# Fewer split units in the last batch, and later summaries by block transposes with a common maximum

## The chip, the cores and the metric

The kernel runs on one core of a Trainium2 chip. The metric is the device time of one execution in microseconds (us); the median of three runs is given.

## What is computed

An attention block with 32 inducing points summarizes each of 4 batches of 12480 tokens, the tokens attend to that summary, and a two-layer network with a squared, clipped activation follows. All in float32, C = 128, d_ff = 2048; the reference, cut:

```python
B, N, m, C = (4, 12480, 32, 128)
def mab(q, kv):
    s = scale * (q @ kv.transpose(0, 2, 1))
    s = s - s.max(-1, keepdims=True)
    a = np.exp(s)
    a /= a.sum(-1, keepdims=True) + 1e-09
    return a @ kv
h = mab(I, x)            # 32 inducing points over all tokens of a batch
x = mab(x, h)            # each token over the 32 rows of h
h = x @ w_in             # 128 -> 2048
g = np.where(h >= 1, h, np.where(h <= -1, 0.0, (h + 1) ** 2 / 4))
out = g @ w_out          # 2048 -> 128
```

## The kernel before

A batch is cut into 26 chunks of 480 tokens, and chunks into groups of four (the seventh group has two). There are three kinds of work.

**Summary of a batch** (`summarize`). For each group PE computes the scores of the 32 points against the chunks' transposed tokens `xT`, four chunks side by side in the 128 partitions of one PSUM bank (`scores`, L554). DVE takes the maximum of each partition (`most`, L559) and scales it (`nb`, L562), ACT takes exponentials with that bias and their sums (`exps`, L571). PE then turns the exponentials in 4 transposes (`turn`, L595), ACT or DVE copies them to `eN` (`put`, L603), and PE multiplies them with the tokens `xn` in 16 tiled matmuls (`weigh`, L611), each chunk for itself; `keep` (L618) stores the 128 x 128 partial results. A short chain (`c1` to `c12`) joins the groups with a weight per partition and group, and `hT`, the summary, is multiplied with `w_in` (L720) into `hw`. Batch 0 is summarized at the start, from tokens that PE transposes itself, in 5 pieces of 96; the summary of batch b+1 is made while batch b's chunks run. There SP loads each chunk twice: as `xn`, and as `xr`, which a DVE block transpose makes into `xT` (L535).

**Attention of the tokens** (`attend`, L765 to L831): scores against `hT`, a softmax by DVE, ACT and POOL, and the weights `a` and their rounded part `ahi` are sent by SP to `aT`, four DMAs per chunk.

**The network** (`chunk`). A chunk has 8 units of 256 hidden columns, each in two PSUM banks of pool `h` (7 banks). Per unit: two hidden matmuls (L953, one pass each, float32r), ReLU on ACT (L961; one wide instruction if both banks are ready and adjacent, or two single ones), square on ACT (L947), the cap on DVE (L966; pair or single). The output matmul (L1053) runs in one of two ways. A *split* unit makes `hi`, a rounded copy of `w` (on DVE L1024, ACT L1021 or POOL L1019, as the planner chooses), and `lo = w - hi` on POOL (L1027), and PE runs three single-pass matmuls per half. Another unit uses `w` itself in a float32 matmul per half, which the trace shows as two records. `SPLIT` names the six split units of a chunk, `END` the five of the last chunk of all. DVE turns the sum (L1065) and SP stores it.

**Order.** No engine's order is written by hand. `Plan.order` runs a list of operations with costs through a model of the engines: at each step an engine takes, of the operations that are ready and whose buffers are free, the one with the lowest due time. Due times are a base (the unit's place times `STEP`) plus an entry of the table `DUE`; `LONE`, `KEEP` and `WAIT` are further constants of that choice, and `SLOTS` gives the number of buffers. The result is a fixed order for each engine's queue. Idle places of PE in the first 73 us of the plan are filled with small matmuls (`keep_on`, L1082). The score bank of a group is one of the seven `h` banks; it is free again after the exponentials:

```python
m = add("PE", 850, 1050, SC[0], scores, [ind_made, *(xT_made[b, c] for c in cs)],
        [p1, e1[g], *(xT[b, c] for c in cs)], tiled=True)
v = add("DVE", 760, 900, SC[1], most, [m, folded, prior], [p1])
mosts.append(v)
e = add("ACT", 645, 780, SC[2], exps, [v], [e1[g], p1])
```

Of the kernel before, what the change touches and what calls it, by code (L numbers as in the profile page):

```python
# [9 lines left out]
F32 = mybir.dt.float32  # L10
# [8 lines left out]

END = (0, 1, 3, 4, 6)  # L20
# [4 lines left out]
    h=7, o=1, xn=9, xT=26, xr=2, e1=1, eN=1, hw=6, hx=1, hy=1, w=8, hi=4, lo=4, aT=3, s2=2, a=1, ahi=1, oT=1  # L25
)

FIRST = ["xn", "w", "xn", "hi", "xn", "w", "xn", "lo", "xn", "w"]
# [22 lines left out]
    "end": [-102350],  # L51
# [19 lines left out]
LONE = {"r": 7750, "t": 3200}  # L71

KEEP = 100

WAIT = 175250
# [177 lines left out]
def attn_moe(  # L253
# [10 lines left out]
    P = 128  # L264
# [19 lines left out]
    SHAPE = [(5, 96)] + [(4, 120)] * (B - 1)  # L284
    x_first = x.rearrange("b (k p t) c -> b k p t c", p=96, t=5)
    x_rows = x.rearrange("b (k t p) c -> b k p t c", p=120, t=4)
# [4 lines left out]
        xn=([96, 5, C], F32), xT=([C, CW], F32),  # L291
# [4 lines left out]
    banks = psum.tile([P, SLOTS["h"] + SLOTS["o"], 512], F32, name="banks")  # L296
    count = [0]

    def make(slot, shape=None, dtype=None):

        count[0] += 1
        if slot.pool in ("h", "o"):
            slot.tile = banks[:, slot.place + (SLOTS["h"] if slot.pool == "o" else 0), :]
            return slot.tile
# [182 lines left out]
    def summarize(b, begin, pace, end):  # L487

        xn, got, e1, eN = {}, {}, {}, {}
        T, TP = SHAPE[b]  # L490
        rows_of = x_rows if b else x_first
        lasts, mosts, summed = [], [], []
        prior = state.get("chain")

        def load(g, due, step):
            for q in range(nqs[g]):
                c = g * Q + q
                due += step
                xT[b, c] = in_turn("xT")

                pool = FIRST[c % len(FIRST)] if b == 0 else "xn"
                xn[c] = in_turn(pool) if pool == "xn" else Slot(pool)
                got[c] = add(
# [4 lines left out]
                if b == 0:  # L508
                    pt = Slot("h")

                    def turn(c=c, pt=pt):
                        p = make(pt)
                        for t in range(T):
                            nc.tensor.transpose(  # L514
                                p[:, t * TP : (t + 1) * TP], xn[c].tile[:, t, :], ident[:TP, :TP]
                            )
# [621 lines left out]
```

## Time and profile before

| | |
|---|---|
| median of 3 runs | 1732.59 us (1731.34 to 1733.43) |
| the profiled execution | 1732.11 us, of which the trace spans 1730.3 |
| busy in the span | PE 1696.6 (98%), ACT 1664.2 (96%), DVE 1626.2 (94%), POOL 1612.6 (93%) |
| granted TensorE clock | 0.999 of full speed |
| DMA | 105.76 MB, mean 61 GB/s |

PE is TensorE's matmuls, PEld its weight loads, DVE VectorE, ACT ScalarE, POOL GpSimd, SP the engine that issues the DMAs, SPq its queue. L12 is line 12 of the kernel. An instruction's duration includes its way through the engine, which the next one overlaps; what an instruction costs a full engine is read from its start to the next one's start. A name such as `w` stands for all buffers of that pool.

### The profile page before, as it was taken

To read this page: it belongs to the slowest core of one execution; us is meant where nothing else is said; L and a number is where in the kernel's file an instruction comes from. 1 tells how busy PE (TensorE), PEld (TensorE's weight loads), DVE (VectorE), ACT (ScalarE), POOL (GpSimd) and SP (SyncE) were. 2 spreads that over 40 slices of the span, in tenths; PEclk is the share of its full clock that TensorE was granted. 3 is DMA by queue.
4 is the path that set the end of the run, shared out by engine and by line. 5 is a ranking of instruction groups with operands and counts; after the bars stand their busy time and mean duration, and the time that the engine had idled before them with its cause. 6 is when DMAs were issued, how large, how long until landed. Compare 5 with 4: busy or idle time off the path is not lost.

```text
span 1730.3 us, 26049 instructions
## 1 busy us (share of the span) xinstructions
PE 1696.6 (98%) x8062; PEld 1229.5 (71%) x8062; DVE 1626.2 (94%) x2167; ACT 1664.2 (96%) x2486; POOL 1612.6 (93%) x875
## 2 busy tenths in 40 slices
PE   6999999999999999999999999999999999999998
PEld 5667777777767777777777777777777677777776
DVE  5799999999999999999999999999999999999997
ACT  5699999999999999999999999999999999999997
POOL 1599999999899999999999999999989999999997
PEclk9999999999999999999999999999999999999999
DMA  9443323333334233343143333232212111111111
GB/s 235 112 74 69 74 58 70 57 62 61 70 66 77 47 72 63 66 75 68 31 93 54 74 68 69 51 66 52 42 34 53 33 30 30 35 35 35 33 31 18
DMA packets 427950, 105.76 MB, mean 61 GB/s; under 512 B 370562, under 2 KB 421218, under 8 KB 427810
## 3 DMA queue, kind: packets, MB, share of 16 engines
q1 hardware_dynamic: 426722, 103.84, 30.5%
q8 instruction: 64, 1.05, 0.3%
q14 instruction: 76, 0.62, 0.1%
q10 hardware_dynamic: 1088, 0.25, 0.1%
HBM read 48.94 MB, written 25.56 MB: 43 GB/s over the span
## 4 chain that ended last, share of the span: by engine, by line
PE 62%; ACT 16%; DVE 11%; issue 5%; POOL 3%; DMA 2%; SPq 1%; DVEq 0%; ACTq 0%; POOLq 0%
PE banks L1053 43%; PE banks L953 14%; ACT w L961 8%; ACT w L947 6%; DVE w L966 6%; DVE hi L1024 3%; POOL lo L1027 2%; PE banks L611 1%; PE banks L765 1%; ACT hi L1021 1%; PE banks L554 1%; SPq L532 1%; DMA xr<-in_x 1%; DVE oT L1065 1%; PE banks L514 1%
## 5 line engine op out<-in xcount | busy, mean ns | idle before, releaser
L1027 POOL TENSOR_TENSOR lo<-w,hi 128x960 fp32r<-128x960 f32 x623 | 1395.9, 2271 | 40.3 <-DVE hi L1024 17.9
L966 DVE SCALAR_TENSOR_TENSOR w<-banks,w 128x480 f32<-128x480 f32 (+1 forms) x1200 | 960.6, 838 | 35.9 <-ACT w L947 30.7
L961 ACT ACTIVATE w<-banks 128x480 f32<-128x480 f32 (+1 forms) x1352 | 843.7, 700 | 15.0 <-PE banks L953 13.9
L947 ACT ACTIVATE w<-w 128x960 f32<-128x960 f32 x832 | 842.2, 1049 | 2.7
L953 PE MATMUL banks<-aT,hw 128*128 128x480 f32 x1664 | 605.6, 432 | 7.3 <-DVE w L966 5.2
L1053 PE MATMUL banks<-hi,w_lo 128*128 128x480 f32 x1246 | 492.0, 395 | 5.4 <-DVE oT L1065 3.3
L1024 DVE TENSOR_REDUCE hi<-w 128x960 fp32r<-128x960 f32 x409 | 464.7, 1142 | 18.2 <-PE banks L1053 1.2
L1053 PE MATMUL banks<-hi,w_hi 128*128 128x480 f32 x1246 | 472.9, 380 | 0.0
L953 PEld LDWEIGHTS banks<-aT,hw 128*128 128x128 f32 x1664 | 304.7, 188 | 167.6 <-DVE w L966 71.1
L1053 PE MATMUL banks<-w,w_f 128*128 128x480 f32 x836 | 391.4, 567 | 0.0
L1053 PE MATMUL banks<-lo,w_hi 128*128 128x480 f32 x1246 | 385.2, 395 | 0.8 <-POOL lo L1027 0.8
L1053 PEld LDWEIGHTS banks<-hi,w_lo 128*128 128x128 f32 x1246 | 234.2, 188 | 76.2 <-DVE oT L1065 18.0
L1053 PEld LDWEIGHTS banks<-lo,w_hi 128*128 128x128 f32 x1246 | 229.8, 188 | 76.2 <-POOL lo L1027 25.7
L1053 PEld LDWEIGHTS banks<-hi,w_hi 128*128 128x128 f32 x1246 | 234.2, 188 | 40.0 <-issue 7.2
L1053 PEld LDWEIGHTS banks<-w,w_f 128*128 128x128 f32 x836 | 155.9, 189 | 68.7 <-issue 50.9
L1019 POOL TENSOR_SCALAR hi<-w 128x960 fp32r<-128x960 f32 x140 | 139.6, 1002 | 19.3 <-DVE w L966 10.4
L1021 ACT CAST hi<-w 128x960 fp32r<-128x960 f32 x74 | 75.5, 1021 | 4.7 <-DVE w L966 3.1
L1065 DVE STREAM_TRANSPOSE oT<-banks 128x480 f32<-128x480 f32 x104 | 70.1, 674 | 7.9 <-PE banks L1053 6.5
L535 DVE STREAM_TRANSPOSE xT<-xr 128x480 f32<-128x480 f32 x78 | 51.2, 659 | 0.0
L808 POOL TENSOR_TENSOR a<-a,ahi 128x480 fp32r<-128x480 f32 (+1 forms) x28 | 34.5, 1232 | 0.6 <-ACT ahi L805 0.6
L441 POOL TENSOR_TENSOR w_in_sb<-hi,lo 128x256 f32<-128x256 f32 x8 | 6.1, 763 | 28.4 <-DVE hi L430 28.4
L611 PEld LDWEIGHTS banks<-xn,eN 120*32 120x32 f32 (+1 forms) x754 | 24.4, 109 | 11.1 <-ACT eN L603 4.4
(107 smaller groups left out, 580.0 us busy)
## 6 DMA issues: line engine op xcount, KB each, us to landing
out<-oT SPq DMA_DIRECT2D x414, 60.0 KB, 2.2
xn<-in_x SPq DMA_DIRECT2D x91, 240.0 KB, 4.2
xr<-in_x SPq DMA_DIRECT2D x312, 60.0 KB, 2.5
aT<-ahi SPq DMA_DIRECT2D x206, 60.0 KB, 2.0
aT<-a SPq DMA_DIRECT2D x206, 60.0 KB, 2.0
w<-in_moe_w_in SPq DMA_DIRECT2D x8, 256.0 KB, 5.7
w<-in_moe_w_out SPq DMA_DIRECT2D x8, 256.0 KB, 3.8
hw<-hy SPq DMA_DIRECT2D x32, 64.0 KB, 2.0
```

What stands on the lines that cost most here:

```text
L535: nc.vector.transpose(make(xT[b, c]), xr.tile.rearrange("c n i -> c (n i)"))
L611: nc.tensor.matmul(p[q * M : (q + 1) * M, :C], eN[g].tile[:, t, q * M : (q + 1) * M], xn[g * Q + q].tile[:, t, :], start=(t == 0), stop=(t ...
L947: nc.scalar.activation(w.tile, w.tile, AF.Square, scale=0.5)
L953: nc.tensor.matmul(make(h)[:, :CW], hw[b][ft // 4].tile[:, ft % 4 * P : (ft % 4 + 1) * P], aT[b, c].tile, start=True, stop=True,)
L961: each(of, i, hs_, lambda h, to: nc.scalar.activation(to, h, AF.Relu, bias=1.0), w)
L966: lambda h, t: nc.vector.scalar_tensor_tensor(h if kept else t, h, 1.0, t, op0=ALU.max, op1=ALU.min), w,
L1019: nc.gpsimd.tensor_scalar(make(hi), w.tile, 1.0, 0.0, op0=ALU.mult, op1=ALU.add)
L1021: nc.scalar.copy(make(hi), w.tile)
L1024: nc.vector.tensor_reduce(make(hi), w.tile.unsqueeze(3), axis=AX.X, op=ALU.max)
L1027: nc.gpsimd.tensor_sub(make(lo), w.tile, hi.tile.bitcast(F32))
L1053: nc.tensor.matmul(acc.tile[:, :CW], wt[k][:, i, :], g.tile[:, i, :], start=first, stop=(acc.parts == 0),)
L1065: nc.vector.transpose(make(oT).rearrange("c n i -> c (n i)"), acc.tile[:, :CW])
```

## The change

1. In the last batch every chunk whose number is odd uses the five split units of `END` and three float32 units (unit 7 is the third). This holds for 13 chunks, of which the last had it before.
2. The later summaries turn the exponentials by 32 x 32 blocks on DVE, from SBUF to SBUF. For that the four chunks of a group must share one maximum per inducing point, since a matmul now sums over all four: DVE's maximum of each partition goes by four small DMAs (`line`) to 32 partitions, DVE takes the maximum of four (`one_most`), and four DMAs (`spread`) bring it back. The tokens are loaded by the same rows as the blocks, four chunks in one tile, and the weighted sum is 15 tiled matmuls.
3. The tokens' buffers: three of 128 x 1920 elements in place of nine of 96 x 640, the first batch's nine lying inside them; loads for later batches wait for the first summary's end.
4. The whole table `DUE` and the constants `LONE`, `KEEP` and `WAIT` have other numbers.

```diff
+LESS = ((), (), (), (1, 3))
 END = (0, 1, 3, 4, 6)
...
-    "h": [-28300, -9600, -120350, -9950, -10750, -3800, -56800, -49450],
+    "h": [-32350, -5700, -18700, -12450, -27300, -2200, -49100, -47200],
...
-LONE = {"r": 7750, "t": 3200}
-KEEP = 100
-WAIT = 175250
+LONE = {"r": 6200, "t": 800}
+KEEP = 800
+WAIT = 210850
...
+                    got[c] = add("SP", 700, 3000, at(due, "x"), fetch, state["first"], [xn[c]])
...
+            def line(q):
+                nc.sync.dma_start(m4[:, q : q + 1], mq[q * M : (q + 1) * M])
+            def one_most():
+                nc.vector.tensor_reduce(m4[:, Q:], m4[:, :nq], axis=AX.X, op=ALU.max)
+            def spread(q):
+                nc.sync.dma_start(mg[q * M : (q + 1) * M, g : g + 1], m4[:, Q:])
...
+                l = [add("SP", 610, 2700, SC[1], lambda q=q: line(q), [v]) for q in range(nq)]
+                v = add("DVE", 75, 215, SC[1], one_most, l)
+                l = [add("SP", 610, 2700, SC[1], lambda q=q: spread(q), [v, prior]) for q in range(Q)]
+                mosts.extend(l)
+                v = add("DVE", 75, 215, SC[1], less, l)
...
+                def over():
+                    to = make(eN[g], [P, NB, M])[:rows].rearrange("p n m -> p (n m)")
+                    nc.vector.transpose(to, e1[g].tile[:rows])
+                def weigh_all():
+                    p = make(ph)
+                    for n in range(NB):
+                        nc.tensor.matmul(
+                            p[n % Q * M : (n % Q + 1) * M, :C], eN[g].tile[:rows, n, :], xn[g * Q].tile[:rows, n, :],
+                            start=n < Q, stop=n >= NB - Q,
+                        )
...
-            split = k in (END if (b, c) == (B - 1, NCH - 1) else SPLIT)
+            split = k in (END if (b, c) == (B - 1, NCH - 1) or c % 4 in LESS[b] else SPLIT)
```

Two places of the order. The first is PE at the end of the first summary, ahead of the turns of its sixth group (`ident` alone: a filler; `ident,e`: the turns; `xT,indT`: the scores of the last group). Before:

```order
L611 MATMUL banks<-xn_435,eN_776 32x128
L611 MATMUL banks<-lo_376,eN_776 32x128
L611 MATMUL banks<-xn_445,eN_776 32x128
L611 MATMUL banks<-w_412,eN_776 32x128
L1082 MATMUL banks<-ident 128x128 x11
L595 MATMUL banks<-ident,e_161_835 96x128 x5
L554 MATMUL banks<-xT_759,indT 32x480
L554 MATMUL banks<-xT_770,indT 32x480
L611 MATMUL banks<-xn_463,eN_851 32x128
```

Changed:

```order
L670 MATMUL banks<-tokens,eN_812 32x128
L670 MATMUL banks<-lo_426,eN_812 32x128
L670 MATMUL banks<-tokens,eN_812 32x128
L670 MATMUL banks<-w_462,eN_812 32x128
L1139 MATMUL banks<-ident 128x128 x21
L655 MATMUL banks<-ident,e_158_893 96x128 x5
L571 MATMUL banks<-xT_795,indT 32x480
L571 MATMUL banks<-xT_806,indT 32x480
L670 MATMUL banks<-tokens,eN_911 32x128
```

Ten more fillers stand between the fifth group's weighted sum and the sixth group's turns; what follows is the same.

The second is DVE around the maximum of the second group of batch 1's summary, made while batch 0 runs (`mg<-banks` and `nb<-mg` before; now `mq<-banks`, and the maximum of four is `m_1_1`). Before:

```order
L1024 TENSOR_REDUCE hi_2037<-w_1985 128x960
L1024 TENSOR_REDUCE hi_2047<-w_1993 128x960
L559 TENSOR_REDUCE mg<-banks 128x1
L562 TENSOR_SCALAR nb_1_120<-mg 128x1
L966 SCALAR_TENSOR_TENSOR w_2021<-banks,w_2021 128x480 x2
L966 SCALAR_TENSOR_TENSOR w_2049<-banks,w_2049 128x960
L1065 STREAM_TRANSPOSE oT_2079<-banks 128x480
L966 SCALAR_TENSOR_TENSOR w_2007<-banks,w_2007 128x480 x2
L1024 TENSOR_REDUCE hi_2096<-w_2049 128x960
L603 COPY eN_2108<-banks 120x512
```

Changed:

```order
L1023 SCALAR_TENSOR_TENSOR w_2002<-banks,w_2002 128x480 x2
L577 TENSOR_REDUCE mq_1_138<-banks 128x1
L1081 TENSOR_REDUCE hi_2059<-w_1986 128x960
L1023 SCALAR_TENSOR_TENSOR w_2033<-banks,w_2033 128x480
L1023 SCALAR_TENSOR_TENSOR w_2048<-banks,w_2048 128x960
L1023 SCALAR_TENSOR_TENSOR w_2033<-banks,w_2033 128x480
L1023 SCALAR_TENSOR_TENSOR w_2071<-banks,w_2071 128x480
L1081 TENSOR_REDUCE hi_2096<-w_2048 128x960
L586 TENSOR_REDUCE m_1_1_139<-m_1_1_139 32x1
L1023 SCALAR_TENSOR_TENSOR w_2071<-banks,w_2071 128x480
L551 STREAM_TRANSPOSE xT_2110<-xr_1927 128x480
L1023 SCALAR_TENSOR_TENSOR w_2087<-banks,w_2087 128x480 x2
```

The scaling, right behind the maximum before, has moved: first comes the maximum of four, six instructions behind, and the scaling stands seven rows further on. The copy of `eN` is gone.

SP's queue at the same place, changed (`aT<-ahi` and `aT<-a`: the loads of a chunk's attention; `out<-oT`: a store):

```order
L1126 DMA out<-oT_1983 480x1x32 x4
L888 DMA aT_2019<-ahi_1943 32x480 x2
L888 DMA aT_2019<-a_1924 32x480 x2
L583 DMA m_1_1_139<-mq_1_138 32x1 x4
L589 DMA mg<-m_1_1_139 32x1 x4
L888 DMA aT_2148<-ahi_1943 32x480
L1126 DMA out<-oT_2139 480x1x32 x4
L888 DMA aT_2148<-ahi_1943 32x480
L888 DMA aT_2148<-a_1924 32x480 x2
```

The eight small DMAs stand between the loads of two chunks' `aT`; there was none of them before.

## Rows read from the trace of the kernel before

**Rows 1.** Busy time by stage: stretch, length, busy us of each engine, PE clock, DMA.
```profile
485.00:902.00 417.00, 414.93 (x1936) 300.48 (x1935) 399.42 (x524) 410.49 (x612) 402.50 (x216) 1.00 0.34 65
...
1319.00:1725.00 406.00, 402.66 (x1631) 291.93 (x1630) 390.68 (x484) 397.96 (x575) 394.79 (x205) 1.00 0.16 31
```

**Rows 2.** Groups by line, PE: line, engine, operation, count | busy us, mean ns | idle before.
```profile
L953 PE MATMUL banks<-aT,hw 128*128 128x480 f32 x1664 | 605.6, 432 | 7.3 <-DVE w L966 5.2 <-ACT e L571 1.0
L1053 PE MATMUL banks<-hi,w_lo 128*128 128x480 f32 x1246 | 492.0, 395 | 5.4 <-DVE oT L1065 3.3 <-ACT w L961 0.4
...
L1053 PE MATMUL banks<-w,w_f 128*128 128x480 f32 x836 | 391.4, 567 | 0.0
```

**Rows 3.** Timeline of PE in the last batch: start us, us from first start to last end.
```profile
1503.66 0.60 PE L1053 MATMUL banks<-lo,w_hi 128*128 128x480 f32 x2
1504.10 0.97 PE L1053 MATMUL banks<-w,w_f 128*128 128x480 f32 x2
1504.53 0.97 PE L953 MATMUL banks<-aT,hw 128*128 128x480 f32 x2
1505.33 0.97 PE L1053 MATMUL banks<-w,w_f 128*128 128x480 f32 x2
```

**Rows 4.** Waits in the last batch: who for whom, us, times, longest.
```profile
PEld banks L953 <- DVE w L966: 21.0, 70, 0.8
```

**Rows 5.** Timeline of POOL in the last batch.
```profile
1498.71 17.93 POOL L1027 TENSOR_TENSOR lo<-w,hi 128x960 fp32r<-128x960 f32 x8
1516.58 1.99 POOL L1019 TENSOR_SCALAR hi<-w 128x960 fp32r<-128x960 f32 x2
```

**Rows 6.** Timeline of DVE in the last batch.
```profile
1499.35 0.68 DVE L1065 STREAM_TRANSPOSE oT<-banks 128x480 f32<-128x480 f32 x1
1499.95 1.19 DVE L966 SCALAR_TENSOR_TENSOR w<-banks,w 128x480 f32<-128x480 f32 x2
1501.06 2.19 DVE L1024 TENSOR_REDUCE hi<-w 128x960 fp32r<-128x960 f32 x2
1503.16 3.32 DVE L966 SCALAR_TENSOR_TENSOR w<-banks,w 128x960 f32<-128x960 f32 x3
1506.40 1.14 DVE L1024 TENSOR_REDUCE hi<-w 128x960 fp32r<-128x960 f32 x1
```

**Rows 7.** Timeline of ACT in the last batch.
```profile
1507.13 0.99 ACT L1021 CAST hi<-w 128x960 fp32r<-128x960 f32 x1
1508.01 1.04 ACT L961 ACTIVATE w<-banks 128x480 f32<-128x480 f32 x2
1508.92 1.02 ACT L947 ACTIVATE w<-w 128x960 f32<-128x960 f32 x1
1509.82 1.46 ACT L961 ACTIVATE w<-banks 128x480 f32<-128x480 f32 x2
```

**Rows 8.** Timeline of PE in a summary of batch 2, made during batch 1.
```profile
543.60 0.60 PE L595 MATMUL banks<-ident,e 128*120 128x128 f32 x4
543.96 0.68 PE L1053 MATMUL banks<-lo,w_hi 128*128 128x480 f32 x2
```

**Rows 9.** Groups by line, ACT: the copies of the turned exponentials.
```profile
L603 ACT COPY eN<-banks 120x512 f32<-120x512 f32 x12 | 7.5, 627 | 0.1
```

**Rows 10.** Timeline of PE at the end of the first summary: fillers.
```profile
48.63 2.72 PE L1082 MATMUL banks<-ident 128*128 128x128 f32 x22
```

**Rows 11.** POOL's L1027 alone: duration in ns, min/median/max.
```profile
L1027 POOL TENSOR_TENSOR lo<-w,hi x623: 2226/2270/2347, 73.9 to 1719.7; 128x960 fp32r<-128x960 f32 x156
```

**Rows 12.** Timeline of all engines: a later group's scores and exponentials.
```profile
513.29 1.01 PE L554 MATMUL banks<-xT,indT 128*32 128x480 f32 x8
...
520.82 0.66 ACT L571 ACTIVATE e<-banks,nb 128x480 f32<-128x480 f32 x1
```

**Rows 13.** The tile `aT` alone: duration in ns of an issue on SP, time to landing.
```profile
L831 SPq DMA_DIRECT2D aT<-ahi x206: 507/588/1911, 82.2 to 1671.8; - x103
...
DMA to landing us min/median/max: 1.9/2.0/3.8
```

More of the change, by code (lines that the diff above doesn't have):

```diff
@@ L296, in attn_moe @@
     banks = psum.tile([P, SLOTS["h"] + SLOTS["o"], 512], F32, name="banks")
+    tokens = work.tile([P, SLOTS["xn"], 3 * 5 * C], F32, name="tokens")
     count = [0]
@@ L303, in make @@
             slot.tile = banks[:, slot.place + (SLOTS["h"] if slot.pool == "o" else 0), :]
+            return slot.tile
+        if slot.pool == "xn":
+            slot.tile = tokens[:, slot.place, :].rearrange("p (n c) -> p n c", n=NB)
+            return slot.tile
+        if slot.pool == "x3":
+            n, k = divmod(slot.place, 3)
+            slot.tile = tokens[:TP, n, k * T * C : (k + 1) * T * C].rearrange("p (t c) -> p t c", t=T)
             return slot.tile
@@ L489, in summarize @@
         xn, got, e1, eN = {}, {}, {}, {}
-        T, TP = SHAPE[b]
-        rows_of = x_rows if b else x_first
         lasts, mosts, summed = [], [], []
         prior = state.get("chain")
+        state.setdefault("first", lasts)
         def load(g, due, step):
@@ L549, in score @@
             nb = small("nb", [P, 1], f"_{b}_{g}")
+            mq, m4 = small("mq", [P, 1], f"_{b}_{g}"), small("m4", [M, Q + 1], f"_{b}_{g}")
             def scores():
@@ L558, in most, with less @@
             def most():
-                nc.vector.tensor_reduce(
-                    mg[:rows, g : g + 1], p1.tile[:rows, :CW], axis=AX.X, op=ALU.max
-                )
+                to = mq[:rows] if b else mg[:rows, g : g + 1]
+                nc.vector.tensor_reduce(to, p1.tile[:rows, :CW], axis=AX.X, op=ALU.max)
+                if b == 0:
+                    less()
+            def line(q):
[4 more added lines that the diff above has]
+                nc.sync.dma_start(mg[q * M : (q + 1) * M, g : g + 1], m4[:, Q:])
+            def less():
                 nc.vector.tensor_scalar(nb[:rows], mg[:rows, g : g + 1], -SCALE, None, op0=ALU.mult)
@@ L568, in exps @@
                 else:
-                    to = make(e1[g])[:rows].rearrange("w (i n) -> w i n", i=M)
-                    of = p1.tile[:rows, :CW].rearrange("w (n i) -> w i n", i=M)
+                    to, of = make(e1[g])[:rows], p1.tile[:rows, :CW]
                 nc.scalar.activation(
@@ L577, in score @@
                     [p1, e1[g], *(xT[b, c] for c in cs)], tiled=True)
-            v = add("DVE", 760, 900, SC[1], most, [m, folded, prior], [p1])
-            mosts.append(v)
+            v = add("DVE", 760 if b == 0 else 690, 900, SC[1], most, [m, folded, prior], [p1])
+            if b == 0:
+                mosts.append(v)
+            else:
+                l = [add("SP", 610, 2700, SC[1], lambda q=q: line(q), [v]) for q in range(nq)]
[3 more added lines that the diff above has]
+                v = add("DVE", 75, 215, SC[1], less, l)
             e = add("ACT", 645, 780, SC[2], exps, [v], [e1[g], p1])
@@ L588, in gather, with keep_all @@
             pe, pf, ph, eN[g] = Slot("h"), Slot("h"), Slot("h"), Slot("eN")
-            to = [pe, pf] if b == 0 else [pe]
+            if b:
+                def over():
[8 more added lines that the diff above has]
+                        )
+                def keep_all():
+                    nc.scalar.copy(hs[:, g, :], ph.tile[:, :C])
+                GA = [at(due, "GA", n) for n in range(4)]
+                v = add("DVE", 600, 735, GA[1], over, [scored], [e1[g], eN[g]])
+                m = add("PE", 880, 1080, GA[2], weigh_all, [v, *(got[g * Q + q] for q in range(nq))],
+                        [ph, eN[g], xn[g * Q]], tiled=True)
+                lasts.append(add("ACT", 150, 290, GA[3], keep_all, [m, folded, prior], [ph]))
+                return
+            to = [pe, pf]
             def turn():
@@ L603, in put @@
                 copy(e[:, :4, :rows], pe.tile[:TP].rearrange("p (t w) -> p t w", w=P)[:, :, :rows])
-                if b == 0:
-                    copy(e[:, 4, :rows], pf.tile[:TP, :rows])
+                copy(e[:, 4, :rows], pf.tile[:TP, :rows])
             def weigh():
@@ L618, in keep @@
                 nc.scalar.copy(hs[:rows, g, :], ph.tile[:rows, :C])
-            GA = [at(due, "GA", n) for n in range(4)] if b else [at(0, "g0", g)] * 4
+            GA = [at(0, "g0", g)] * 4
             each_ = 110 if nq == Q else 85
@@ L623, in gather @@
             when = GA[1]
-            by = dict(DVE=(615, 750, when), ACT=(485, 620, when))
-            if b == 0:
-                by = dict(ACT=(660, 800, when) if nq == Q else (430, 570, when))
+            by = dict(ACT=(660, 800, when) if nq == Q else (430, 570, when))
             v = add(by, 0, 0, 0, put, [m], [eN[g], *to])
```

32 lines of the change are left out of this document (17 added, 15 removed), and 46 rows, old and new, of the table DUE.

## The prediction

> **What bounds the kernel now.** I read the busy times by stage first. From the first hidden matmul to the last output transpose the program runs its four batches back to back, and in each of them every engine is nearly full [rows 1]: in batch 1 ACT is busy 410.5 of 417 us, and in the last batch PE 402.7, ACT 398.0, POOL 394.8 and DVE 390.7 of 406. So no single engine is the bound; four queues in a fixed order hold each other up. A matmul counts as busy while it waits behind another, so for PE I counted work instead. The counts stand in the groups by line [rows 2], the durations in the timeline, read from one start to the next: two single-pass matmuls take 0.44 us, so 0.22 each; a float32 matmul, which the trace shows as two records, and two single-pass ones behind it take 1.23 us, so 0.79 for the float32 one [rows 3]. With 1664 hidden and 3 x 1246 split ones (1188 us), 418 float32 ones (330 us) [rows 2] and, by my estimate, 85 us of scores, summaries and chain, PE has about 1603 us of work in the 1657 us from 68 to 1725. It loses some 54 us, 13 per batch. The wait table names whom it waits for: in the last batch above all DVE's cap of `w` (21 us of idle weight loads) [rows 4], the instruction that frees a bank.
>
> **The change, engine by engine.** The instruction order of the changed kernel was counted for this; the durations are the trace's.
>
> *Three float32 units instead of two, in 12 chunks of the last batch* (chunk 25 had five split units before). Each unit trades 6 single-pass matmuls (1.32 us) for 2 float32 ones (1.58) [rows 3]: PE +0.26 x 12 = **+3.1 us**. Each unit loses its `lo` on POOL, 8 of which go back to back in 17.87 us, so 2.23 each, and its `hi` copy. The order shows 12 fewer `lo`, and of the `hi` copies DVE has 25 fewer, ACT 4 more, POOL 9 more. POOL: -12 x 2.23 + 9 x 1.0 = **-17.8** [rows 5]. DVE: -25 x 1.05 = -26.3 [rows 6]. ACT: +4 x 0.88 = +3.5 [rows 7]. Nearly all of it lies in the last batch: there DVE loses 19 copies (-20), POOL -26.8 + 8 = -19, ACT 2 copies (-1.8).
>
> *Summaries of batches 1 to 3.* The 84 PE transposes go: four take 0.36 us to the next start [rows 8], so PE **-7.6 us**, 2.5 in each of batches 0 to 2, where these summaries are made. The weighted sum has 15 matmuls for a full group instead of 16, as before in tiles of four: nothing. The 21 copies of `eN` go: 12 on ACT, 0.63 us long [rows 9], of which the next instruction waits some 0.48 (a ReLU of 480 columns, of nearly the same length, takes 0.455 [rows 7]): ACT -5.8; 9 on DVE, at the same price -4.4. DVE gets 21 block transposes: the output transpose of the same size takes 0.60 to the next start [rows 6], +12.6. It also gets 21 small maxima on 32 partitions; their nearest row is much bigger, so I take 0.1 each with ends 0 and 0.6 (0 to 12 us), +2.
>
> *The order as a whole.* ACT has 32 more paired ReLUs in place of 64 single ones. A single one takes 0.455, a 960-column square 0.90 [rows 7], so -0.3. DVE has 35 more pairs for 70 caps: a pair 1.08, a single 0.56 [rows 6], -1.4.
>
> The sum: PE -4.5, ACT -2.6, DVE -18, POOL -18 us. Only DVE and POOL gain much, and both in the last batch; the two engines that are fullest hardly change. So I don't pass the sum on, but stage by stage:
>
> - Last batch: PE's own work grows by 3.1. Its 13 us of lost time should shrink, since those it waits for get 19 and 20 us of room in 406. I take half of it back, -6.5; ends 0 and -12. Net **-3.4**.
> - Batches 0 to 2: PE -2.5 and ACT about -1 each, DVE about +1, POOL the same. I pass on 1.5 per batch, **-4.5**; ends 0 and -7.5.
> - Start: PE gets ten more fillers ahead of the last turns of batch 0, and DVE decodes more weights ahead of that group's maximum. Eleven fillers (22 records) cover 2.7 us [rows 10], so at most +2.5; later in the same chain DVE has fewer decodes between (14 instructions instead of 22 from the last group's maximum to `hT`), which gives some back. I take **+1**; ends 0 and +2.5.
>
> That is -6.9 from the profiled run's 1732.1, 1725.2; the runs' median is 0.5 above the profiled run, so **1726 us**. About 0.2%, 3.5 us, is what a measurement of this kernel can tell from no change.
>
> What I cost at nothing, and its cover. SP issues 162 more DMAs. They stand in its order queue with the loads of `aT`, and the second trip's four wait for DVE's small maximum; behind them stand the loads of `aT` for the next chunk. The plan puts them a chunk ahead of their use. If that cover is gone, the hidden matmuls wait, and ACT with them. On DVE the small maximum and the scaling each wait for a DMA trip; in the piece of order shown six instructions of other work, some 5 us, stand ahead of the small maximum, more than the 4.4 us of four issues and a landing [rows 13], and if one is late, the caps behind it are, and PE's banks. The score bank is also held longer, the same rival.
>
> The Trainium skill speaks against the new transposes: "SBUF — State Buffer" (Terms) has VectorE and GpSimd share a port pair that is held for a whole instruction, the loser blocking fully. This case's rows: 623 `lo` on POOL last between 2.226 and 2.347 us, with DVE copies and transposes from SBUF running beside most of them [rows 6, 11]. A blocked one would be longer by a DVE instruction, 0.6 at least. By the rule POOL would get 21 x 0.6 = 12.6 us in batches 0 to 2, by the rows nothing; the sum goes by the rows.
>
> **The rivals.**
>
> 1. *The room is not used.* PE and ACT are the fullest, and nothing is taken off them in the last batch. Then PE adds its 3.1, lost time gives back 2, the earlier batches 0.5 each, and the start costs 2: +1.6, about 1734 against the median, within the noise. For it: ACT's busy 398 of 406 and that its work there falls by only 1.8. Against it: what PE waits for is DVE [rows 4], which gets the room.
>
> 2. *All the lost time comes back.* In the last batch 12 of 13, +3.1 for PE, so -8.9; the earlier batches pass on PE's whole 2.5 each, -7.5; the start nothing: 1716. For it: the caps that PE waits for stand behind DVE's `hi` copies, 19 of which go. Against it: the earlier batches keep DVE, ACT and POOL as full as they are.
>
> 3. *The bank of the scores (slower).* Before, in the group shown, a bank was held from the scores at 513.3 to the exponentials' end at 521.5 us, 8.2 us [rows 12]. Now two DMA trips stand between the maximum and the exponentials: four issues of 0.6 us each and 2.0 to the landing [rows 13], twice, about 9 us more, 21 times: 190 us in which six banks instead of seven feed the hidden matmuls. If throughput fell with the banks, by a seventh, that would cost 27 us; if two units in flight suffice, nothing. Half is 13: 1739. It decides where ACT begins to wait for hidden matmuls: in batch 1 it idles 6.5 of 417 us altogether [rows 1]; with over 10 us of such waits per batch it has won. For it: ReLU and square of one unit stand next to each other on ACT more often in the new order, 34 instead of 22 times in batch 1, which is what a queue looks like that finds little else ready. Against it: seven banks make three pairs and one odd one, and the odd one may be all that is lost.
>
> 4. *POOL is locked out by the new transposes*: +12.6 on POOL in batches that have no room there, 1738. The range of `lo` [rows 11] is against it. This is the SBUF page's rule of above.
>
> That the change doesn't do what it says is ruled out by the order: unit 7 has 26 float32 matmuls instead of 2, and no transpose is left in the later summaries.
>
> **How the numbers follow.** Forecast 0.50 (1720 to 1729), rival 1 0.23, rival 2 0.10, rival 3 0.14, rival 4 0.03. Faster by over 0.2% (below 1729.1): the forecast and rival 2, 0.60. Same (1729 to 1736): rival 1, 0.23. Slower: rivals 3 and 4, 0.17. The range from 1714 to 1738 leaves out the far half of rival 2 and most of rivals 3 and 4. The range of the likeliest sign alone is 1714 to 1729.
>
> **What will show it.** Right: in the last batch DVE's busy time falls by some 15 to 20 us for the same chunks, POOL's by as much, PE's waits for the cap of `w` fall by half, and the batch (first hidden matmul of batch 3 to the last output transpose, 406 us) takes about 403. Batches 0 to 2 take 415 to 416 instead of 417 each, and the first hidden matmul starts at 69 instead of 68.3. Wrong: if the last batch doesn't shorten although DVE idles, ACT and PE alone set it (rival 1); if batches 1 and 2 get longer and ACT waits for hidden matmuls, the bank was the price (rival 3); if `lo` gets a second, longer duration, the port (rival 4).

## The result, and the profile after

The changed kernel takes **1739.63 us** (median of 5 runs, 1738.84 to 1741.13), the kernel before 1732.59 beside it: 1.0042 of the time before, 95% interval 1.0032 to 1.0053. It is slower by 7 us, where 6.6 us faster was forecast, and the time lies above the range.

Where the 7 us lie is read from starts in the timeline. Every trace begins at a slightly different moment, so all is counted from the first maximum of the first summary. "hT" is VectorE's copy of `hT`, "hidden" the first hidden matmul, "o1" the first output transpose (the end of chunk 0), o26, o52, o78 and o104 the last ones of the four batches. The rows of the runs further down stand in the same table.

| kernel | median us | max to hT | hT to hidden | hidden to o1 | o1 to o26 | to o52 | to o78 | to o104 |
|---|---|---|---|---|---|---|---|---|
| before | 1732.59 | 41.8 | 7.0 | 25.6 | 403.5 | 416.6 | 416.3 | 394.7 |
| changed | 1739.63 | 44.9 | 7.9 | 30.6 | 403.5 | 415.2 | 416.0 | 395.5 |
| e1 | 1739.32 | 44.4 | 7.9 | 29.2 | 404.2 | 415.7 | 415.8 | 395.0 |
| e2 | 1736.42 | 41.8 | 7.0 | 25.6 | 403.7 | 416.4 | 416.6 | 398.7 |
| e3 | 1735.12 | 44.4 | 7.9 | 27.4 | 403.0 | 416.1 | 415.3 | 395.1 |
| e4 | 1735.11 | 44.4 | 7.2 | 26.3 | 403.1 | 416.1 | 416.4 | 394.0 |
| e5 | 1746.01 | 44.4 | 7.6 | 27.6 | 409.2 | 417.9 | 415.5 | 397.5 |
| e6 | 1765.71 | 42.2 | 8.0 | 28.1 | 418.1 | 420.2 | 425.4 | 398.8 |
| e7 | 1741.03 | 42.0 | 11.9 | 30.0 | 404.5 | 414.9 | 415.4 | 395.4 |
| e8 | 1736.97 | 42.0 | 11.7 | 27.7 | 401.5 | 414.8 | 415.4 | 394.9 |
| e9 | 1738.63 | 44.4 | 7.9 | 29.1 | 403.1 | 415.4 | 415.5 | 395.6 |
| e10 | 1735.75 | 42.0 | 8.0 | 28.7 | 404.7 | 415.7 | 415.6 | 395.1 |
| e11 | 1733.80 | 42.0 | 8.0 | 26.8 | 403.5 | 415.0 | 415.4 | 395.0 |
| e12 | 1731.06 | 42.1 | 7.0 | 25.6 | 403.2 | 416.3 | 416.1 | 394.2 |
| e13 | 1737.90 | 44.4 | 7.9 | 26.9 | 406.0 | 415.7 | 415.8 | 395.3 |
| e14 | 1733.80 | 42.2 | 7.0 | 27.7 | 403.8 | 414.7 | 415.5 | 395.3 |
| e15 | 1734.18 | 42.0 | 7.0 | 27.3 | 404.7 | 414.6 | 415.5 | 395.3 |
| e16 | 1733.29 | 42.0 | 7.0 | 27.3 | 404.8 | 414.7 | 415.5 | 395.0 |

In the changed kernel 8.9 us are lost before o1: 3.1 up to `hT`, 0.9 up to the first hidden matmul, 5.0 in the first chunk. After it the program is 1.0 us shorter, not the 8 that the forecast's stages come to without the start. These are stages of one trace each. e1 has the changed kernel's program up to the last batch, and its trace shows 44.4 up to `hT` and 29.2 in the first chunk, so a stage can differ by some 1.4 us from one execution to the next.

**The last batch.** Busy time by stage of the changed kernel, columns as in [rows 1]:
```profile
494.00:908.00 414.00, 411.40 (x1905) 295.77 (x1904) 396.44 (x518) 408.26 (x587) 401.74 (x216) 1.00 0.34 65
1324.00:1732.00 408.00, 404.65 (x1609) 288.52 (x1608) 375.06 (x462) 397.13 (x576) 378.15 (x201) 1.00 0.16 31
```
VectorE (third) is busy 375.1 us instead of 390.7, GpSimd (fifth) 378.2 instead of 394.8, near what was worked out, and the stretch is no shorter: from the first hidden matmul of batch 3 to the last output transpose, as the prediction measured it, 408.6 us instead of 406.5. PE has 2.0 us more. Two waits there (who for whom, us, times, longest; L947 and L1004 are ACT's square), the first row from the kernel before, the other two from the changed one:
```profile
DVE w L966 <- ACT w L947: 3.4, 10, 0.7
DVE w L1023 <- ACT w L1004: 18.7, 32, 1.5
PEld banks L1010 <- DVE w L1023: 18.7, 56, 1.0
```
The weight loads' wait for VectorE's cap fell from 21.0 [rows 4] to 18.7 only. Over the whole program VectorE now idles 60.9 us ahead of its cap (35.9 before), mostly for ACT's square (52.2 of it, before 30.7). The room is there; it is spent on waiting.

**The start.** VectorE in the kernel before (maximum of the sixth group, copy of `hT`), then in the changed one:
```profile
50.06 0.65 DVE L559 TENSOR_REDUCE mg<-banks 128x1 f32<-128x480 f32 x1
61.31 0.19 DVE L698 COPY hT<-banks 128x32 f32<-128x32 f32 x1 [0.74 <-PE banks L694]
```
```profile
52.58 0.65 DVE L577 TENSOR_REDUCE mg<-banks 128x1 f32<-128x480 f32 x1
63.62 0.19 DVE L755 COPY hT<-banks 128x32 f32<-128x32 f32 x1 [1.97 <-PE banks L751]
```
Counted from the first maximum, the sixth comes at 33.8 us instead of 30.5: the lateness is there at the sixth maximum. Ahead of it VectorE is at work, not waiting: between the fifth and the sixth maximum it runs 26 instructions instead of 19, in 11.1 us instead of 8.2, and idles 1.5 us in both. On PE the changed kernel then runs attend scores ahead of the first hidden matmuls:
```profile
70.56 1.01 PE L822 MATMUL banks<-xT,hT 128*32 128x480 f32 x8
71.50 1.79 PE L1010 MATMUL banks<-aT,hw 128*128 128x480 f32 x6
```

**The first chunk.** SyncE's queue in the kernel before, then in the changed one (start, us, what it issues):
```profile
93.53 1.26 SPq L831 DMA_DIRECT2D aT<-ahi  x2
94.83 1.30 SPq L831 DMA_DIRECT2D aT<-a  x2
```
```profile
94.48 1.20 SPq L888 DMA_DIRECT2D aT<-ahi  x2
95.78 2.59 SPq L548 DMA_DIRECT2D xr<-in_x  x4
98.42 1.25 SPq L888 DMA_DIRECT2D aT<-a  x2
```
Four loads of `xr` have come between: the reads of `a` go out 3.9 us behind those of `ahi`, where it was 1.3. There is one buffer `a`. VectorE in the changed kernel, with the idle time ahead and its releaser at the end:
```profile
97.90 0.65 DVE L1023 SCALAR_TENSOR_TENSOR w<-banks,w 128x480 f32<-128x480 f32 x1
101.47 0.68 DVE L859 STREAM_TRANSPOSE a<-s 128x480 f32<-128x480 f32 x1 [2.92 <-DMA aT<-a]
102.07 0.64 DVE L1122 STREAM_TRANSPOSE oT<-banks 128x480 f32<-128x480 f32 x1
```
The next turn into `a` waits for those reads, and the first output transpose stands behind it in the queue. In the kernel before the two stood the other way round, and the wait was shorter:
```profile
93.91 0.62 DVE L1065 STREAM_TRANSPOSE oT<-banks 128x480 f32<-128x480 f32 x1
97.68 0.68 DVE L802 STREAM_TRANSPOSE a<-s 128x480 f32<-128x480 f32 x1 [0.84 <-DMA aT<-a]
```
In e1's trace, with the same order, the wait is 1.61 us, so its length varies. PE needs that transpose, since the accumulator has one bank:
```profile
98.61 0.48 PE L1010 MATMUL banks<-aT,hw 128*128 128x480 f32 x1
102.77 0.77 PE L1110 MATMUL banks<-hi,w_lo 128*128 128x480 f32 x1 [3.68 <-DVE oT L1122]
...
103.73 0.60 PE L1110 MATMUL banks<-hi,w_lo 128*128 128x480 f32 x1
104.14 0.60 PE L1110 MATMUL banks<-hi,w_hi 128*128 128x480 f32 x1
```
After the idle stretch the matmuls start 0.41 us apart, where 0.22 is usual [rows 3]. The same stretch by windows, columns as in [rows 1], with the granted clock third from the end:
```profile
98.00:100.00 2.00, 0.94 (x3) 0.23 (x2) 0.55 (x1) 1.69 (x4) 2.00 (x2) 1.00 0.63 106
100.00:102.00 2.00, 0.00 (x0) 0.00 (x0) 0.53 (x1) 0.00 (x0) 2.00 (x1) 0.59 0.64 186
102.00:104.00 2.00, 1.23 (x3) 1.09 (x4) 2.00 (x5) 1.82 (x3) 1.20 (x2) 0.50 0.95 223
104.00:106.00 2.00, 2.00 (x6) 1.65 (x6) 2.00 (x4) 1.48 (x3) 0.37 (x2) 0.50 0.65 100
106.00:108.00 2.00, 2.00 (x8) 1.67 (x8) 2.00 (x4) 1.25 (x3) 1.97 (x1) 0.70 0.19 31
108.00:110.00 2.00, 2.00 (x11) 1.76 (x10) 1.11 (x3) 2.00 (x3) 1.64 (x1) 1.00 0.25 62
```
The clock went to its lower level, 1.2 GHz, while PE stood idle, and was back at 2.4 by 108. In the kernel before it stayed at 1.00 from 92 to 108.

### The profile page after: what moved, and what is told of

The parts are those of the page before. It is cut to its first block, busy times and chain, and to the rows that moved or that the text cites. A ratio compares the mean times of both kernels' runs of the same rounds, so it can differ in the third digit from the quotient of the medians.

```text
span 1737.4 us, 26007 instructions
## 1 busy us (share of the span) xinstructions
PE 1695.6 (98%) x7970; PEld 1218.1 (70%) x7970; DVE 1609.1 (93%) x2141; ACT 1664.7 (96%) x2446; POOL 1595.8 (92%) x871
## 3 DMA queue, kind: packets, MB, share of 16 engines
q1 hardware_dynamic: 399632, 103.87, 30.5%
## 4 chain that ended last, share of the span: by engine, by line
PE 65%; ACT 14%; DVE 11%; issue 4%; DMA 2%; SPq 2%; POOL 1%; DVEq 0%; ACTq 0%; POOLq 0%
PE banks L1110 46%; PE banks L1010 14%; ACT w L1018 7%; ACT w L1004 6%; DVE w L1023 5%; DVE hi L1081 2%; POOL lo L1084 1%; PE banks L571 1%; DVE oT L1122 1%; PE banks L635 1%; PE banks L822 1%; ACT hi L1078 1%; SPq L548 1%; DMA aT<-a 0%; PE banks L1139 0%
## 5 line engine op out<-in xcount | busy, mean ns | idle before, releaser
L1084 POOL TENSOR_TENSOR lo<-w,hi 128x960 fp32r<-128x960 f32 x611 | 1371.2, 2272 | 55.3 <-DVE hi L1081 23.4
L1023 DVE SCALAR_TENSOR_TENSOR w<-banks,w 128x480 f32<-128x480 f32 (+1 forms) x1165 | 959.0, 859 | 60.9 <-ACT w L1004 52.2
L1004 ACT ACTIVATE w<-w 128x960 f32<-128x960 f32 x832 | 838.0, 1035 | 4.1
L1010 PE MATMUL banks<-aT,hw 128*128 128x480 f32 x1664 | 573.5, 418 | 8.2 <-DVE w L1023 6.6
L1110 PE MATMUL banks<-hi,w_lo 128*128 128x480 f32 x1222 | 512.8, 420 | 11.8 <-DVE oT L1122 8.3
L1110 PE MATMUL banks<-hi,w_hi 128*128 128x480 f32 x1222 | 464.4, 380 | 0.0
L1081 DVE TENSOR_REDUCE hi<-w 128x960 fp32r<-128x960 f32 x384 | 436.7, 1142 | 15.0 <-PE banks L1110 1.3
L1110 PE MATMUL banks<-w,w_f 128*128 128x480 f32 x884 | 411.4, 565 | 0.0
L1110 PE MATMUL banks<-lo,w_hi 128*128 128x480 f32 x1222 | 398.8, 400 | 1.3 <-POOL lo L1084 1.3
L1110 PEld LDWEIGHTS banks<-hi,w_lo 128*128 128x128 f32 x1222 | 229.7, 188 | 109.3 <-issue 33.8
L1110 PEld LDWEIGHTS banks<-w,w_f 128*128 128x128 f32 x884 | 166.1, 188 | 66.7 <-issue 46.5
L1076 POOL TENSOR_SCALAR hi<-w 128x960 fp32r<-128x960 f32 x149 | 148.5, 1001 | 16.1 <-DVE w L1023 4.1
L450 POOL TENSOR_TENSOR w_in_sb<-hi,lo 128x256 f32<-128x256 f32 x8 | 6.1, 763 | 27.6 <-DVE hi L439 27.6
L571 PE MATMUL banks<-xT,indT 128*32 128x480 f32 x208 | 29.0, 593 | 0.0
```

Of the source, the lines that this page charges most:

```text
L571: nc.tensor.matmul(p[q * M : (q + 1) * M, :CW], indT, xT[b, c].tile, start=True, stop=True)
L1004: nc.scalar.activation(w.tile, w.tile, AF.Square, scale=0.5)
L1010: nc.tensor.matmul(make(h)[:, :CW], hw[b][ft // 4].tile[:, ft % 4 * P : (ft % 4 + 1) * P], aT[b, c].tile, start=True, stop=True,)
L1023: lambda h, t: nc.vector.scalar_tensor_tensor(h if kept else t, h, 1.0, t, op0=ALU.max, op1=ALU.min), w,
L1076: nc.gpsimd.tensor_scalar(make(hi), w.tile, 1.0, 0.0, op0=ALU.mult, op1=ALU.add)
L1081: nc.vector.tensor_reduce(make(hi), w.tile.unsqueeze(3), axis=AX.X, op=ALU.max)
```

## The experiments

Each was timed beside the kernel before (4 to 11 runs), on the same chip as the others of its group of four (e1 to e4, e5 to e8 and so on); that kernel's medians were 1732.38 to 1732.73. Times of two of these kernels are compared by their medians. The intervals against the kernel before reach some 1.5 us to either side with ten or eleven runs and 2 to 3 us with fewer, so a difference of 1 us between two of these kernels is not told from none.

**e1 and e2: the float32 units.** e1 takes them out of the changed kernel, e2 puts them alone into the kernel before.
```diff
-LESS = ((), (), (), (1, 3))
+LESS = ((), (), (), ())
```


> The changed kernel with six split units and two float32 units in every chunk of the last batch again; all else, the table of due times too, stays changed. Theory A (the float32 units add 3.1 us of matmuls to the fullest engine and nobody uses the room that they leave on VectorE and GpSimd): the last batch takes 406.5 us from its first hidden matmul to the last output transpose instead of 408.5, first hidden matmul 71.5 and first output transpose 102.1 as in the changed kernel, total 1737.5, 1.003 of the kernel before. Theory B (the forecast: room on VectorE and GpSimd gives back more than the 3.1): last batch 411 to 412, total 1743.

> The kernel before with three float32 units in every second chunk of the last batch, and nothing else of the change. Theory A: last batch 408.5 us instead of 406.4, all earlier stages as before, total 1734.6, 1.001 of the kernel before. Theory B (the forecast): last batch 403, total 1729, 0.998.

e1 takes 1739.32 us, 0.3 under the changed kernel; its last batch is 0.5 shorter. e2 takes 1736.42, 1.0026 of the kernel before (1.0017 to 1.0035), and all of it lies in the last batch, 398.7 for 394.7. The units show no gain. Under the old table they cost 4 us, more than PE's 3.1; under the new one the 0.3 is within the noise. Neither theory's numbers were met; e2's sign was theory A's, and theory B's gain of 3 to 4 us is in neither run. From the first hidden matmul e1's last batch still takes 408.2 us, so most of the 2.1 us that it grew by (406.5 to 408.6) is not the units'.

**e3 and e12: two buffers `a`, in turn, in the order as it is;** in the changed kernel (e3) and in the one before (e12).
```diff
         s, d = FORM[slot.pool]
+        if slot.pool == "a":
+            slot.place = slot.turn % 2
```


> The changed kernel with two buffers for the attention tile a, used in turn; the order of the instructions is the same. Theory A (in the first chunk VectorE's in-order queue stands 2.9 us at the turn back into a, until the transfers aT<-a have read it; PE starves behind it and its granted clock falls): that wait is gone, first output transpose at 99 instead of 102.1, clock at 100 to 108 near 1.00, total 1735, 5 us under the changed kernel. Rival (the next thing, the single buffer of the upper half, is as late): first output transpose at 101 to 102, clock still down, total 1739.

> Control: the kernel before with two buffers a used in turn, the same order. Theory A (its order has aT<-a directly behind aT<-ahi, so that little waits for the single a): 1732, within 1 us of the kernel before, first chunk 25 to 25.6. Rival (the single a costs in every chunk, whatever the order): 1729 or less.

VectorE in e3:
```profile
98.34 0.65 DVE L1025 SCALAR_TENSOR_TENSOR w<-banks,w 128x480 f32<-128x480 f32 x1
98.90 0.67 DVE L861 STREAM_TRANSPOSE a<-s 128x480 f32<-128x480 f32 x1
99.50 0.64 DVE L1124 STREAM_TRANSPOSE oT<-banks 128x480 f32<-128x480 f32 x1
```
The 2.92 us are gone, and e3 takes 1735.12, as theory A said: 4.5 us under the changed kernel for one buffer. This is the largest single step. But the first chunk is still 1.8 us longer than before, and the clock still falls (0.72 at 100 to 102, 0.50 at 102 to 104). e12 takes 1731.06, 0.9989 of the kernel before (0.9980 to 0.9998), with no stage over 0.6 us shorter, between the two theories: the wait costs little in the old order. e12 is the fastest kernel of the study, if by little.

**e4: the tokens held back, alone.** In the kernel before the token loads of later batches wait for the first summary's end, as the shared memory makes them do in the changed one.
```diff
+        state.setdefault("first", lasts)
...
-lambda c=c: nc.sync.dma_start(make(xn[c], [TP, T, C], F32), rows_of[b, c]), [], [xn[c]],
+lambda c=c: nc.sync.dma_start(make(xn[c], [TP, T, C], F32), rows_of[b, c]), state["first"] if b else [], [xn[c]],
```


> The kernel before, in which the token loads of batches 1 to 3 may only start behind the end of the first summary, as in the changed kernel; nothing else of the change. Theory A (holding them pulls the loads of w_out and their decoding ahead of the first summary's last maxima): first hidden matmul at 71 to 71.5 instead of 68.3, total 1735 to 1736, 1.002 of the kernel before; if the first chunk's stall comes from it too, first output transpose at 100 or later and total 1739. Rival (the new table of due times makes the start late): first hidden matmul at 68 to 69, total 1732.6.

It takes 1735.11, 1.0014 of the kernel before (1.0006 to 1.0023). From the first maximum to `hT` it needs 44.4 us, as e1, e3, e5, e9 and e13 do, against 41.8: +2.6, and its time is up by 2.7. Theory A holds: the late start comes from the held tokens, under the old table and with the old summaries. They empty SyncE's queue, the sixth load of `w_out` lands 26.8 us behind the first maximum instead of 30.1, and VectorE, in the order, has 95 instructions ahead of the sixth maximum instead of 88: more decoding of weights. The first chunk's stall does not come from here (26.3).

**e5 and e6: the table.** e5 is the changed code with the old `DUE`, `LONE`, `KEEP` and `WAIT`, e6 the old code with the new ones.

> The code of the changed kernel with the table of due times, LONE, KEEP and WAIT of the kernel before. In its order the transfers aT<-a follow directly on aT<-ahi, as before. Theory A (start late because tokens are held; the first chunk's stall comes from the new table's order on SyncE): from the first maximum to the first hidden matmul 52.3 us as in the changed kernel (before 48.8), from the first hidden matmul to the first output transpose 26 to 27.5 (changed 30.6, before 25.6); the float32 chunks cost their 4 us in the last batch as they did under the old table; total 1738. Rival (the stall comes with the new summaries themselves): 30 us again for the first chunk, total 1742.

> The code of the kernel before with the new table of due times, LONE, KEEP and WAIT; four float32 transposes per summary group and early tokens stay. In its order four transfers xr<-in_x stand between aT<-ahi and aT<-a in the first chunk, as in the changed kernel. Theory A: first maximum to first hidden matmul 49 to 50 us, first hidden matmul to first output transpose 29 to 31 (the stall and the lower clock are there), total 1736 to 1738. Rival (the stall needs the new summaries or the late tokens): 25.6 to 26.5 for the first chunk, total 1733.

e5 takes 1746.01, e6 1765.71 (1.0187, 1.0170 to 1.0204). Both totals are missed by far: batch 0 alone grows to 409.2 and 418.1. A table fits its own code. The first chunk without the new table is 27.6 (theory A's 26 to 27.5, just missed), and 28.1 in e6 is between both theories. The changes of order are too many to read more from the times. But the traces settle which part of the change brought the wait at `a`. VectorE in e6, the old code with the new table, then in e5, the new code with the old table:
```profile
97.32 0.68 DVE L802 STREAM_TRANSPOSE a<-s 128x480 f32<-128x480 f32 x1 [1.78 <-DMA aT<-a]
```
```profile
102.40 0.67 DVE L859 STREAM_TRANSPOSE a<-s 128x480 f32<-128x480 f32 x1
```
In e6 the first output transpose stands right behind that turn, as in the changed kernel, and PE waits 2.36 us for it; in e5 it stands ahead (at 98.50), and the turn does not wait. The stall comes with the new table, not with the new summaries.

**e7, e9 and e10: the start.** e7 ties the loads of `w_out` to chunk 25's tokens instead of chunk 21's; e9 lets the later tokens go only behind the spreads of `hw`; e10 does both.
```diff
-        made, f = load_f32(src, when, due, after=got_all[0, 21])
+        made, f = load_f32(src, when, due, after=got_all[0, 25])
...
-... fetch, state["first"], [xn[c]])
+... fetch, [*state["first"], *(o for h in hw_made[0] for o in h)], [xn[c]])
```


> The changed kernel, in which the loads of w_out wait for the last token load of batch 0, not for the 22nd of 26. In its order VectorE has 13 instructions fewer ahead of the sixth maximum (82 instead of 95), and 8 fewer ahead of the seventh. Theory A (those decodes made the start late): first maximum to first hidden matmul 49.5 to 50 us instead of 52.3 to 52.7, first chunk's stall as it was, total 1737. Rival (the weights are then missing in the first chunk): first hidden matmul to first output transpose 32 or more instead of 30, total 1740.

> The changed kernel, in which the token loads of batches 1 to 3 also wait until the spreads of hw of batch 0 have been made; the rest of the order on the engines is the same. Theory A (beside the late decodes, seven token loads of 240 KB right ahead of the spreads of hw on the same queue hold these up): from the copy of hT to the first hidden matmul 7.0 us as before, instead of 7.9; first maximum to first hidden matmul 51.5; the first chunk as in the changed kernel, 29 to 30.6; total 1738.5. Rival (the token transfers also slow the loads of aT in the first chunk): first chunk 26 to 28, total 1735 to 1736.

> The kernel of e9 with the loads of w_out behind the last token load of batch 0 too, as in e7. Theory A: both causes of the late start are gone, first maximum to first hidden matmul 49 to 49.5 us (before 48.8, changed 52.5, e7 53.9), first chunk 29 to 30, total 1736. Rival (e7's long issues of hw have another cause than the token loads): 53 to 54 again, total 1740.

The expectations of e7 and e10 take chunk 25's load for the last and the loads of `w_out` for later. In the order chunk 25 goes out ahead of 21 (due -24600 and -13900 in the table), and the first load of `w_out` is issued 7.9 us behind the first maximum instead of 11.3, so earlier. What did change is VectorE's order: in the traces 81 instructions stand ahead of the sixth maximum instead of 94, and it comes at 27.9 us instead of 33.8. So e7, and e8, e10 and e11 with it, test the decodes ahead of the maximum, and not late loads.

e7 brings `hT` back to 42.0, and is slower: 1741.03. Two spreads now hold SyncE for 6.2 us, right behind seven loads of tokens:
```profile
59.05 3.45 SPq L522 DMA_DIRECT2D tokens<-in_x  x7
64.53 6.22 SPq L797 DMA_DIRECT2D hw<-hx  x2
70.85 2.84 SPq L797 DMA_DIRECT2D hw<-hy  x4
```
In e10, without the tokens ahead, two take 1.2:
```profile
63.97 1.23 SPq L797 DMA_DIRECT2D hw<-hx  x2
65.30 2.44 SPq L797 DMA_DIRECT2D hw<-hy  x4
```
e10 takes 1735.75, 2.9 under e9 and 3.9 under the changed kernel. But in the changed kernel itself the tokens are through in time: e9 has the same 7.9 us from `hT` to the first hidden matmul, and theory A's second half falls; its time, 1738.63, is within the noise of the changed kernel's. The 0.9 is the attend scores' (e14).

**e8 and e11: repairs together.** e8 is e7 with two `a`, e11 is e10 with two `a`.

> The changed kernel with both repairs: the later loads of w_out and two buffers a. If start and first chunk are the whole loss and the repairs add up: first maximum to first output transpose 77 us instead of 83.3 (before 74.4), total 1732.5, the time of the kernel before. If they cover the same time: 1735.

> The kernel of e10 with two buffers a. If start, spreads and the single a are the whole loss: first maximum to first output transpose 76 to 77 us (before 74.4, changed 83.3), total 1731 to 1732.5, level with the kernel before or up to 1.5 us under it. If a fourth cause stands behind: 1735.

e8 takes 1736.97 (e7's spreads again), e11 1733.80, 1.0009 of the kernel before (1.0001 to 1.0018). From the changed kernel the steps are 1.0 us for the tokens behind the spreads (e9, within the noise), 2.9 for the decodes (e9 to e10) and 2.0 for `a` (e10 to e11); a little more than 1 us to the kernel before is left. The repairs partly cover the same time: the second `a` is worth 4.5 us in the changed kernel and 4.1 in e7 (e8), but 2.0 here.

**e13 to e16: one or two instructions moved in the finished order.** e13 puts the first output transpose of the changed kernel ahead of the turn into `a`; e14 puts e11's first attend scores and their transpose behind two hidden matmuls; e15 does both in e11; e16 is e15 without the float32 chunks. The edit is e15's; e14 has it without the last two lines, e13 has those two alone.
```diff
     done = plan.order()
+    of = lambda part: [n for n, op in enumerate(done) if op.emit.__qualname__.endswith(part)]
+    late = of("chunk.<locals>.hidden")[1]
+    for part in ("turn", "scores"):
+        done.insert(late, done.pop(of("attend.<locals>." + part)[0]))
+        late -= 1
+    first = of("chunk.<locals>.turn")[0]
+    done.insert(first, done.pop([n for n in of("attend.<locals>.back") if n < first][-1]))
```


> The changed kernel, in whose finished order one instruction moves: on VectorE the first output transpose goes ahead of the turn back into a instead of behind it. Theory A (the wait for the single a costs through the output transpose queued behind it, for which TensorE's next projections wait): first output transpose at 98.6 to 99.5 us instead of 102.1, TensorE's clock falls for a shorter time or not, total 1736 to 1737. Rival (the caps that are still queued behind a starve TensorE just as long): the output transpose is early, but the second output transpose comes at 119 us as before and the total is 1739.5.

> The kernel of e11, in whose finished order the first attend scores on TensorE and their transpose on VectorE go behind the first two hidden matmuls. Theory A: from the copy of hT to the first hidden matmul 7.0 us instead of 7.95, total 1733.0, 0.8 under e11. Rival (aT of the next chunk is then as much later): total 1733.8 as e11.

> The kernel of e11 with both moves, of e13 and of e14. If they are the rest of the loss: first maximum to first output transpose 75 to 75.5 us (before 74.4, e11 76.8), TensorE's clock without a fall at the end of the first chunk, total 1732, level with the kernel before. If not: 1733.5.

> The kernel of e15 with two float32 units in every chunk of the last batch again. Theory A (under the new table they are worth next to nothing either way, 0.3 us in e1): within 0.7 us of e15. Rival (the forecast): 3 us slower than e15.

e13 takes 1737.90, 1.7 under the changed kernel, between the two theories. VectorE:
```profile
98.05 0.68 DVE L1122 STREAM_TRANSPOSE oT<-banks 128x480 f32<-128x480 f32 x1
100.91 0.68 DVE L859 STREAM_TRANSPOSE a<-s 128x480 f32<-128x480 f32 x1 [2.18 <-DMA aT<-a]
101.51 2.31 DVE L1023 SCALAR_TENSOR_TENSOR w<-banks,w 128x480 f32<-128x480 f32 x4
```
The output transpose is early, but the caps now stand behind `a`, and PE waits 1.83 us for them. Whatever is queued behind the single buffer pays.

e14 has the 7.0 us of the kernel before from `hT` to the first hidden matmul, and the same time as e11, 1733.80: the 0.9 is lost again by o1 (27.7 instead of 26.8 in the first chunk, a difference within that of one trace). e15, 1734.18, gains nothing either, and its clock still falls to 0.50 at 98 to 100; both theories of a gain fall. e16, 1733.29, is 0.9 under e15, with intervals that overlap (1.0003, 0.9994 to 1.0012, against 1.0009, 1.0000 to 1.0017): the rival, 3 us slower, falls for good.

**What stays open.** e15 reaches its first hidden matmul as early as e12, and is 1.7 us later at o1. Part of that may be order: in the new one 28 hidden matmuls stand ahead of o1 instead of 26. Between 70 and 135 us PE's waits sum to 4.6 us in e15 and 3.7 in the kernel before, and its mean clock there is 0.97 instead of 1.00. e11 shows such a fall of the clock too, without any long stall. PE in e11, then in e14:
```profile
96.33 0.70 PE L1112 MATMUL banks<-lo,w_hi 128*128 128x480 f32 x2 [1.09 <-POOL lo L1086]
97.00 0.48 PE L1012 MATMUL banks<-aT,hw 128*128 128x480 f32 x1
98.14 0.48 PE L1112 MATMUL banks<-hi,w_lo 128*128 128x480 f32 x1 [0.67 <-DVE oT L1124]
```
```profile
96.36 0.71 PE L1112 MATMUL banks<-lo,w_hi 128*128 128x480 f32 x2 [1.08 <-POOL lo L1086]
98.19 0.49 PE L1112 MATMUL banks<-hi,w_lo 128*128 128x480 f32 x1 [0.66 <-DVE oT L1124]
```
The windows behind these waits, again e11 and then e14:
```profile
98.00:100.00 2.00, 1.86 (x6) 1.54 (x7) 2.00 (x5) 2.00 (x4) 2.00 (x2) 0.65 0.92 239
100.00:102.00 2.00, 2.00 (x7) 1.65 (x6) 1.93 (x3) 2.00 (x4) 2.00 (x3) 0.50 1.02 227
```
```profile
98.00:100.00 2.00, 1.81 (x8) 1.56 (x9) 2.00 (x5) 2.00 (x4) 2.00 (x2) 1.00 0.78 215
100.00:102.00 2.00, 2.00 (x11) 1.59 (x11) 1.92 (x3) 2.00 (x4) 2.00 (x3) 1.00 0.97 215
```
The same two waits, for GpSimd's `lo` and for the output transpose, stand ahead of a fall in e11 and of none in e14, and both kernels take 1733.80. So these waits alone don't decide the fall, and the fall doesn't account for the rest of the loss: in e15 it comes at 97.8, behind o1 (96.3), and the six of e15's eleven runs with a mean clock of 1.0 have a median of 1733.5, still some 0.8 over the kernel before. What the last 1 us is stays open.

## Why the prediction was wrong

- **The start, "+1; ends 0 and +2.5".** It measured +3.9 to the first hidden matmul (+3.5 in e1's trace), outside the ends. The mechanism was named (more decoding ahead of the late maxima), the size was not: I priced the fillers, and set the 14 instead of 22 instructions behind the last maximum against the rest. The last maximum came 3.4 us later, and only 0.3 came back behind it. That the scores stand ahead of the hidden matmuls I did not see; by e14's time they cost nothing that shows. Why more is decoded there was not in the prediction: the held token loads (e4).
- **"What I cost at nothing": the loads of `aT`.** This is the step that failed worst: the first chunk took 5.0 us more (3.6 in e1's trace), and taking the wait away gave 4.5 (e3). I named the cover, a chunk ahead of use, and looked only at the new transfers of the summaries. What came between were four `xr` loads, and who waited was not the hidden matmul but VectorE, for the buffer that those transfers read; the output transpose stood behind it, and PE behind that. All of this could be read in the order of the changed program: the `xr` loads between `ahi` and `a`, and the output transpose behind the turn. It is the new table's doing (e5, e6); the prediction's term for the order as a whole counted pairs only.
- **The last batch, "half is taken back", -3.4.** The engine sums were right in sign and near in size: VectorE -15.6 (worked out -20), GpSimd -16.6 (-19), PE +2.0 (+3.1). The step from room to time was wrong: what came back of PE's lost time was less than its new work, and the stage grew by 2.1 by the prediction's own measure (0.7 between output transposes). e2 shows that the units cost 4 us under the old table; e1 and e16 show no gain under the new one, where the difference is within the noise. That is rival 1 for this stage, and its reason (ACT and PE are the fullest) fits the rows: VectorE now waits for ACT's square. That the square is what holds the batch was not tried.
- **Batches 0 to 2, "1.5 each".** Batch 1 gave 1.4, batch 2 0.3, batch 0 nothing behind o1. Over the kernels with the changed code and table batch 1 took 414.7 to 416.1 and batch 2 415.3 to 416.0: 0.5 to 1.9 and 0.3 to 1.0 less. Right in sign, about half in size or less. No run has the new summaries alone, so what of the change this gain comes from is not shown.
- **Rival 3 (the bank)** had the slower sign and nearly the time, 1739 (its 13 us on top of the forecast's gains), by the wrong mechanism: batches 1 and 2 got shorter, and ACT idled 5.7 us in batch 1 instead of 6.5. That it came near is luck. **Rival 4** falls: 611 `lo` last 2.214 to 2.349 us (before 2.226 to 2.347 [rows 11]), with 21 block transposes more on VectorE, and the 23 that ran beside one of these 2.236 to 2.346. The blocking that the Trainium skill's "SBUF — State Buffer" (Terms) describes does not show in these rows.

## What to carry to other kernels

Room on an engine that isn't the last to finish bought nothing here: before taking back "half of the lost time", ask who the freed engine waits for next. Where each stage gains a microsecond at most, the fill before the steady state decides, so walk it instruction by instruction in the new order: for every single buffer, find the instruction that refills it, the transfer that must have read it, and what is queued behind. A table of due times tuned for one code can't be judged on another code: swapped, it cost 6 to 33 us.

## What the runs showed of the hardware

- In the changed kernel's trace the clock fell to 0.50 during a wait of PE of 3.7 us, and behind it matmuls of 480 columns came 0.41 us apart instead of 0.22: the stall also slowed what came after it. A long wait is not needed: e11's clock fell to 0.50 behind waits of 1.09 and 0.67 us. Nor do such waits make it sure: behind the same two in e14, and behind one of 1.06 us in the kernel before, it stayed at 1.00.
- Two 64 KB issues 2.0 us behind the last of seven of 240 KB held SyncE's queue 6.2 us (e7); with 4.3 us between them, in the changed kernel, two took 1.6, and with no token loads ahead (e10) 1.2.
- The span's start is loose: the first maximum came 18.4 to 20.6 us after it, so stages were compared from that maximum.
